# Sinkhorn attention, Fourier mixing and MLP on one core: V cast by its load, f16 means, contiguous e-1 reads, no gate before batch 1, bounded reordering

## The chip, the cores and the metric

The kernel runs on one core of a Trainium2 chip. The metric is the device time in microseconds (us) of one execution. Fast runs of one kernel on one chip mostly agree within 1%. A run that is over 1.5% above the fastest of its kernel is called slow and is not used in a comparison.

TensorE is called PE in the profile (PEld is its weight load), VectorE is DVE, ScalarE is ACT, GpSimd is POOL. "L258" is line 258 of that kernel's own source, so the same operation has different line numbers in different kernels.

## The reference, cut to what matters

```python
# B=4 batches, H=8 heads, S=768 positions, D=64, 8 blocks of 96
P = sort_net
for _ in range(5):                                   # Sinkhorn
    P = np.exp(P - P.max(-1, keepdims=True))
    P = P / P.sum(-1, keepdims=True)
    P = P / P.sum(-2, keepdims=True)
k_sorted = einsum('bhij,bhjcd->bhicd', P, k_blocks)  # blocks mixed by P
v_sorted = einsum('bhij,bhjcd->bhicd', P, v_blocks)
attn = softmax(q_block @ k_sorted_block.T / 8)       # inside each block
x = (attn @ v_sorted)                                # -> [B, 768, 512]
u = x + real(fft(fft(x, axis=1), axis=2))            # over positions, then columns
un = (u - mean(u)) / sqrt(var(u) + 1e-6)
out = u + relu(un @ w1) @ w2                         # 512 -> 2048 -> 512
```

(... the normalisers' 1e-9 and the casts are cut.)

## The kernel before

All of it is one instruction stream that Python generators record piece by piece; a scheduler then orders the instructions on each engine. One generator does the attention of the four batches, one the FFT and normalisation, one the MLP, and one prepares V of batches 2 and 3. V is handled by pairs of batches: 128 partitions are 2 batches x 8 heads x 8 blocks.

The kernel attends with e-1 in place of e = exp(score) and adds V's mean back by other paths, so it needs, for each pair of batches, V in f16 (`vcx`) and the sum of V over the 96 keys of a block ("the means").

V of the first pair comes as f32 over the sync queue, is summed by f32 matmuls and cast by ScalarE:

```python
v32 = [...]                                   # two f32 tiles, 48 keys each
for n in range(4):
    hf, qq = divmod(n, 2)
    start(nc.sync.dma_start(v32[hf][:, 24 * qq:24 * qq + 24, :],
                            vv[0:128, 24 * n:24 * n + 24, :]))
vcx = const.tile([128, 128, D], F16, name="vcx")
dtab = vcx[:, 96:112, :]...                   # a table lives in vcx's spare rows
vcp = vcx[:, 0:BLK, :].rearrange("p (r c) d -> p c r d", r=6)

def v_mean0(n):                               # 12 of these
    nc.tensor.matmul(psm..., idf, v32[n // 6][...], start=(n == 0), stop=(n == 11))

def v_cast(src, n):                           # 8 of these
    nc.scalar.copy(vcp[:, 2 * n:2 * n + 2], src.rearrange("p (c r) d -> p c r d", r=6))
```

The second pair is loaded later, again as f32, cast by ScalarE and summed by VectorE:

```python
def v1_gen():
    for hf in range(2):
        sv = wt([128, 48, D], F32, "hrB", 1, "v32")
        start(nc.gpsimd.dma_start(sv, vv[128:256, 48 * hf:48 * hf + 48]))
        ...
        for n in range(4):
            v_cast(sv[:, 12 * n:12 * n + 12, :], 4 * hf + n)
        ...                                   # VectorE halves sv by additions
    vb_make(1, ...)
    ...
    for n in range(16):
        v_mix(1, n)                           # the second mixing
```

The scores of a block pair are exponentiated into `ex`, and e-1 is written from there into the tile that the next matmul reads. `ex` is in one key order, the destination in another, so e-1 reads `ex` in steps of 16 elements:

```python
nc.scalar.activation(ex..., pss[h2]..., AF.Exp, scale=SCALE)
src = ex.rearrange("p j r c -> p j c r")
if pick(t, 0.5, 0.5) == "DVE":
    nc.vector.tensor_scalar(ed, src, -1.0, None, op0=ALU.add)
else:
    nc.scalar.activation(ed, src, AF.Identity, bias=negone[0:96])
```

A gate holds batch 1's attention until batch 0's second half is normalised:

```python
def attn_gen(k0):
    for b in range(B):
        while b == 1 and not gate1():         # gate1(): (0, 1) in uns
            yield None
        yield from attn(b, k0 if b == 0 else None)
```

One load that turns out to matter is in both kernels: `lt2`, a table of 97 partitions of 3 KB, comes over the sync queue with the other tables, after the Sinkhorn's sixth step.

```python
start(nc.sync.dma_start(tab, ...)); start(nc.sync.dma_start(dtab, ...))
start(nc.sync.dma_start(cs, ...))
lt2 = const.tile([97, 2, S], F16, name="lt2")
start(nc.sync.dma_start(lt2, cn["lt"].ap()))
```

The softmax here doesn't subtract the row's maximum and nothing guards it: scores larger than these inputs give would overflow.

Of the kernel before, what the change touches and what calls it, by code (L numbers as in the profile page):

```python
# [20 lines left out]
D = 64  # L21
# [79 lines left out]
def kernel(  # L101
# [98 lines left out]
    load_qk(0, 0)  # L200
    load_qk(0, 1)
    pack = const.tile([128, 240], F32, name="pack")
# [9 lines left out]

    vv = v.rearrange("b h (i c) d -> (b h i) c d", i=NB)
    v32 = []
    for hf in range(2):
        v32.append(wt([128, 48, D], F32, "hr" + "AB"[hf], 1, "v32"))
    for n in range(4):
        hf, qq = divmod(n, 2)
        start(nc.sync.dma_start(v32[hf][:, 24 * qq:24 * qq + 24, :],
                                vv[0:128, 24 * n:24 * n + 24, :]))  # L220

    vcx = const.tile([128, 128, D], F16, name="vcx")
    dtab = vcx[:, 96:112, :].rearrange("p (c w) d -> p c (w d)", c=4)
    vcp = vcx[:, 0:BLK, :].rearrange("p (r c) d -> p c r d", r=6)

# [7 lines left out]
    for n in range(NKS):  # L233
        t = const.tile([128, NB, 8, 16], F16, name=f"ksb{n}")
        start(nc.gpsimd.memset(t[:, :, 6:8, :], 0.0))
        ksb.append(t)
# [17 lines left out]
    pwt = pw.rearrange("p i j -> p j i")  # L254
    psm = pm([128, 8, D])

    def v_mean0(n):
        nc.tensor.matmul(  # L258
            psm.rearrange("p c d -> p (c d)"), idf,
            v32[n // 6][:, 8 * (n % 6):8 * (n % 6) + 8, :].rearrange(  # L260
                "p c d -> p (c d)"), start=(n == 0), stop=(n == 11))
        op("PE", 0.86)

    def v_cast(src, n):
        nc.scalar.copy(vcp[:, 2 * n:2 * n + 2],  # L265
                       src.rearrange("p (c r) d -> p c r d", r=6))
        op("ACT", 0.86, clk["PE"])

    def v_cast0(n):
        hf, qq = divmod(n, 4)  # L270
        v_cast(v32[hf][:, 12 * qq:12 * qq + 12, :], n)

# [9 lines left out]

    for n in range(6):
        v_mean0(n)

    ph = []
    for it in range(5):
        if it == 0:
            nc.vector.tensor_reduce(rmax, pw, axis=AX.X, op=ALU.max)
            nc.vector.tensor_tensor(  # L290
                pw, pw, rmax[:, :, None].broadcast_to([32, NB, NB]),
                op=ALU.subtract)
        nc.scalar.activation(pw, pw, AF.Exp)
        if it > 1:
            v_cast0(it - 2)
        for src, bc in ((pw, rs[:, :, None]), (pwt, rs[:, None, :])):
            nc.vector.tensor_reduce(rs, src, axis=AX.X, op=ALU.add)
            nc.vector.reciprocal(rs, rs)
            ph.append(nc.vector.tensor_tensor(
                pw, pw, bc.broadcast_to([32, NB, NB]), op=ALU.mult))  # L300
# [29 lines left out]
    def make_bdk(b):  # L330
# [15 lines left out]
        pw[:, :, None, :].broadcast_to([32, NB, 16, NB]))  # L346
    q_copy(0, 0)
    psk = pm([128, NB, 32])
    for i in range(NB):
# [15 lines left out]
    def kq(b, hp):  # L365
# [4 lines left out]
        for half in range(2):  # L370
            ps = pf([128, 3, 128])
            for r3 in range(3):
                r = 3 * half + r3
                for h2 in range(2):
                    nc.tensor.matmul(
                        ps[64 * h2:64 * h2 + 64, r3, :],
                        k16[:, 2 * hl + h2, r, :],
                        bdk[b][:, 2 * hp + h2].rearrange("p i c -> p (i c)"))
            t = op("PE", 0.2)
            t1 = evac(ks[:, :, 3 * half:3 * half + 3, :].rearrange(  # L380
                "p i r c -> p r i c"),
                ps.rearrange("p r (i c) -> p r i c", c=16), t, 384)
        qr, tq = qrs[b, hp]
# [10 lines left out]
    def scores(ks, qt, g, es):  # L394
        pss = [pf([128, 4, BLK]) for _ in range(2)]
        for j in range(4):
            cc = slice(16 * (4 * g + j), 16 * (4 * g + j) + 16)
            for h2 in range(2):
                rows = slice(64 * h2, 64 * h2 + 64)
                nc.tensor.matmul(  # L400
                    pss[h2][:, j, :],
                    ks[rows, 4 * g + j].rearrange("p r c -> p (r c)"),
                    qt[rows, :, cc])
        t = op("PE", 0.36)
        exs = []
        for h2 in range(2):
            ex = wt([96, 4, 6, 16], F32, "ex", 3)
            nc.scalar.activation(
                ex.rearrange("p j r c -> p (j r c)"),
                pss[h2][0:96].rearrange("p j q -> p (j q)"), AF.Exp,  # L410
                scale=SCALE)
            exs.append((ex, op("ACT", 0.5, t)))
        ts = []
        for h2 in range(2):
            e = es[h2]
            ed = bass.AP(
                tensor=e.tensor, offset=e[:, S * g:S * g + 1].offset,
                ap=[e[0:96, :].ap[0], [224, 4], [6, 16], [1, 6]])
            ex, t = exs[h2]
            src = ex.rearrange("p j r c -> p j c r")  # L420
            if pick(t, 0.5, 0.5) == "DVE":
# [354 lines left out]
    def mlp(b):  # L776
        for g in range(2):
# [3 lines left out]
            yield max(t, 62.0)  # L781
            if (b, g) == (0, 1):
                while not v1ok[0]:
                    yield None
            hr = wt([128, 16, GT], F16, "hr" + "AB"[g], 1)
            for fc in range(16):
# [88 lines left out]

    v1ok = [False]

    def v1_gen():
        part = const.tile([128, 2, 3, D], F32, name="vpart")
        for hf in range(2):  # L880
            sv = wt([128, 48, D], F32, "hrB", 1, "v32")
            start(nc.gpsimd.dma_start(sv, vv[128:256, 48 * hf:48 * hf + 48]))
            while clk["PE"] < 62.0 + 8.0 * hf:
                yield None
            for n in range(4):
                v_cast(sv[:, 12 * n:12 * n + 12, :], 4 * hf + n)
                yield clk["PE"] + 0.8
            w = 24
            while w > 3:
                nc.vector.tensor_tensor(sv[:, 0:w], sv[:, 0:w],  # L890
                                        sv[:, w:2 * w], op=ALU.add)
                op("DVE", 0.1 + w * D / 960.0, clk["PE"])
                w //= 2
                yield clk["PE"] + 0.8
            nc.vector.tensor_tensor(part[:, hf], sv[:, 0:3], sv[:, 3:6],
                                    op=ALU.add)
        vb_make(1, part.rearrange("p a c d -> p (a c) d"))
        op("DVE", 0.9)
        v1ok[0] = True
        while 1 not in attnd:  # L900
# [19 lines left out]

    def gate1():
        m = 3
        return (True, (0, 0) in uns, 0 in rowsd, (0, 1) in uns, ndone[0] >= 1,
                ndone[0] >= 3, ndone[0] >= 5, ndone[0] >= 6)[m]

    ndone = [0]

    def attn_gen(k0):
        for b in range(B):
            while b == 1 and not gate1():  # L930
                yield None
            yield from attn(b, k0 if b == 0 else None)
# [17 lines left out]
    for n in range(6, 12):  # L950
        v_mean0(n)
    for n in range(3, 8):
        v_cast0(n)
    k0[0] = sc(k0[0])
# [27 lines left out]
    with ExitStack() as later:  # L982
        for ins in last.values():
            later.enter_context(tc.issue_after(ins))
        go()


# [28 lines left out]
```

## Time and profile before

| | before |
|---|---|
| time, median of 3 runs (range) | 348.93 us (346.69 to 351.01) |
| span of the profiled run | 345.4 us |
| PE busy | 302.8 us (88%) |
| DVE / ACT busy | 208.1 us (60%) / 149.3 us (43%) |

The table of stretches of the kernel before gives, for each stretch (start:end, length), the busy time of each engine and its number of instructions, then the granted TensorE clock as a share of full speed, the busy share of the DMA engines (over 1 where packets overlap) and GB/s:

```profile
...
core 0: us, PE busy (x) PEld busy (x) DVE busy (x) ACT busy (x) POOL busy (x), PEclk, DMA share, GB/s
60.00:80.00 20.00, 10.47 (x90) 7.70 (x90) 14.48 (x29) 8.67 (x16) 0.58 (x2) 0.75 0.75 172
80.00:100.00 20.00, 12.79 (x60) 7.08 (x59) 14.36 (x30) 8.58 (x13) 3.68 (x9) 0.73 0.22 79
100.00:120.00 20.00, 20.00 (x169) 10.73 (x168) 10.66 (x22) 10.82 (x23) 1.62 (x2) 1.00 0.32 53
...
```

From 100 us on PE has almost no gap; in the 40 us before that it works 10 to 13 us of every 20, at a clock of about 0.74. What must change to save time is before 100 us.

The timeline of the kernel before shows that early chain. Columns: start, duration, engine, line, operation, output<-inputs, shape, count, and in brackets the idle time before it with what ended it:

```profile
...
22.40 7.04 PE L258 MATMUL pm_110<-v_81,pack 128*128 128x512 f32 x12
...
29.38 0.21 PE L400 MATMUL pf_229<-qt_216,ksb_92 64*128 64x96 f16 x1
...
73.32 3.03 ACT L265 CAST vcx<-v_530 128x768 f16<-128x768 f32 x4 [6.57 <-DMA v_530<-in_v_dram]
...
76.89 0.49 ACT L678 ACTIVATE y_833<-pf_826 128x386 f16<-128x386 f32 x1
...
87.08 3.03 ACT L265 CAST vcx<-v_901 128x768 f16<-128x768 f32 x4 [8.54 <-DMA v_901<-in_v_dram]
...
90.01 0.81 ACT L715 ACTIVATE un_951<-u_883,nm_915,ny_914 128x512 f16<-128x512 f32 x1
...
95.41 1.49 PE L789 MATMUL pm_1000<-ut_946,w1sb 128*128 128x384 f16 x4
...
```

The second six f32 means (7.04 us; the trace has two records for each of these matmuls) stand in PE's queue directly before the first scores (29.38). Later ScalarE's queue stands 6.57 us at a cast that waits for the second V load; behind it, in the same queue, is the copy of batch 0's first spectrum (76.89). It stands again, 8.54 us, for the other half, ahead of batch 0's first normalised tile (90.01). The first MLP matmul starts at 95.41.

### The profile page before, as it was taken

To read this page: it belongs to the slowest core of one execution; us is meant where nothing else is said; L and a number is where in the kernel's file an instruction comes from. 1 tells how busy PE (TensorE), PEld (TensorE's weight loads), DVE (VectorE), ACT (ScalarE), POOL (GpSimd) and SP (SyncE) were. 2 spreads that over 40 slices of the span, in tenths; PEclk is the share of its full clock that TensorE was granted. 3 is DMA by queue.
4 is the path that set the end of the run, shared out by engine and by line. 5 is a ranking of instruction groups with operands and counts; after the bars stand their busy time and mean duration, and the time that the engine had idled before them with its cause. 6 is when DMAs were issued, how large, how long until landed. Compare 5 with 4: busy or idle time off the path is not lost.

```text
span 345.4 us, 5986 instructions
## 1 busy us (share of the span) xinstructions
PE 302.8 (88%) x2444; PEld 185.7 (54%) x2444; DVE 208.1 (60%) x453; ACT 149.3 (43%) x275; POOL 35.6 (10%) x71
## 2 busy tenths in 40 slices
PE   1758877457399999999999999999999999999995
PEld 0335866344265477876665655765465455554552
DVE  6432678947855468767368754788451374673641
ACT  2345746350746359997743964505016012120000
POOL 7201104000110110012100100020010010010000
PEclk9968799868589999999999999999999999999999
DMA  7999923935000715060921021002102102212002
GB/s 224 337 244 180 181 47 40 225 161 184 0 0 2 134 53 91 2 94 3 134 77 42 3 47 61 32 0 47 61 32 47 61 32 46 81 33 86 31 2 91
DMA packets 26580, 28.05 MB, mean 81 GB/s; under 512 B 10964, under 2 KB 21716, under 8 KB 26294
## 3 DMA queue, kind: packets, MB, share of 16 engines
q0 software_dynamic: 11424, 13.63, 22.0%
q1 hardware_dynamic: 15128, 14.04, 12.9%
q8 instruction: 19, 0.31, 0.4%
q14 instruction: 9, 0.07, 0.1%
HBM read 29.10 MB, written 6.29 MB: 102 GB/s over the span
## 4 chain that ended last, share of the span: by engine, by line
issue 47%; PE 28%; DMA 12%; POOL 5%; DVE 3%; ACT 3%; POOLq 0%; DVEq 0%; ACTq 0%
DMA q_72<-in_q_dram 5%; DMA v_530<-in_v_dram 4%; PE pm_110 L258 2%; DMA v_901<-in_v_dram 2%; ACT vcx L265 1%; PE pm_4048 L806 1%; PE pm_3673 L806 1%; PE pm_4010 L806 1%; PE pm_3856 L806 1%; PE pm_3643 L806 1%; PE pm_3509 L806 1%; PE pm_4029 L806 1%; PE pm_3894 L806 1%; PE pm_3875 L806 1%; PE pm_3479 L806 1%
## 5 line engine op out<-in xcount | busy, mean ns | idle before, releaser
L789 PEld LDWEIGHTS <-w1sb 128*128 128x128 f16 x512 | 49.1, 99 | 34.7 <-issue 4.6
L496 PEld LDWEIGHTS <-vcx 128*128 128x128 f16 x128 | 20.0, 172 | 0.9
L445 PEld LDWEIGHTS <-eb_87 97*128 97x128 f16 x384 | 17.8, 97 | 2.6 <-ACT eb_87 L425 0.8
L258 PE MATMUL pm_110<-v_80,pack 128*128 128x512 f32 x12 | 7.8, 816 | 7.3 <-DMA v_80<-in_v_dram 7.3
L258 PEld LDWEIGHTS pm_110<-v_80,pack 128*128 128x128 f32 x12 | 3.1, 271 | 11.1 <-issue 11.1
L498 PEld LDWEIGHTS <-vbn_309 128*128 128x128 f16 x64 | 8.6, 135 | 0.8 <-DVE vbn_309 L487 0.4
L498 PEld LDWEIGHTS <-vbn_957 128*128 128x128 f16 x64 | 8.3, 130 | 0.3
L806 PEld LDWEIGHTS <-hrB_3913 128*128 128x128 f16 x48 | 4.7, 98 | 5.5
L806 PEld LDWEIGHTS <-hrA_3749 128*128 128x128 f16 x48 | 4.7, 98 | 5.5
L806 PEld LDWEIGHTS <-hrB_3545 128*128 128x128 f16 x48 | 4.7, 98 | 5.5
L806 PEld LDWEIGHTS <-hrA_3276 128*128 128x128 f16 x48 | 4.7, 97 | 5.6
L806 PEld LDWEIGHTS <-hrB_3069 128*128 128x128 f16 x48 | 4.7, 98 | 5.4
L806 PEld LDWEIGHTS <-hrB_1521 128*128 128x128 f16 x48 | 4.6, 99 | 5.4 <-issue 0.2
L400 PEld LDWEIGHTS <-ksb_94 64*128 64x128 f16 x128 | 4.2, 99 | 5.7 <-issue 2.2
L806 PEld LDWEIGHTS <-hrA_2438 128*128 128x128 f16 x48 | 4.5, 98 | 5.0
L806 PEld LDWEIGHTS <-hrA_999 128*128 128x128 f16 x48 | 4.5, 97 | 5.0
L258 PE MATMUL pm_110<-v_81,pack 128*128 128x512 f32 x12 | 7.0, 748 | 0.0
L265 ACT CAST vcx<-v_901 128x768 f16<-128x768 f32 x4 | 3.0, 828 | 8.5 <-DMA v_901<-in_v_dram 8.5
L732 PE MATMUL pf_960<-pack,un_951 128*128 128x128 f16 x4 | 0.6, 307 | 6.4 <-ACT un_951 L715 6.4
L400 PEld LDWEIGHTS <-ksb_92 64*128 64x128 f16 x128 | 3.7, 94 | 4.4 <-issue 3.4
L890 DVE TENSOR_TENSOR v_530<-v_530 128x1536 f32<-128x1536 f32 (+2 forms) x3 | 3.3, 1087 | 4.4 <-ACT vcx L265 4.4
L798 ACT ACTIVATE hrB_3913<-pm_3914 128x384 f16<-128x384 f32 x1 | 0.5, 491 | 12.5 <-PE pm_3914 L789 12.5
(1310 smaller groups left out, 864.6 us busy)
## 6 DMA issues: line engine op xcount, KB each, us to landing
w1sb<-in_moe_w_ch_dram POOLq DMA_DIRECT2D x4, 512.0 KB, 26.7
w2sb<-in_moe_w_ch_dram POOLq DMA_DIRECT2D x4, 512.0 KB, 14.8
v_80<-in_v_dram SPq DMA_DIRECT2D x2, 768.0 KB, 5.5
v_81<-in_v_dram SPq DMA_DIRECT2D x2, 768.0 KB, 11.5
v_530<-in_v_dram POOLq DMA_DIRECT2D x1, 1536.0 KB, 13.3
v_901<-in_v_dram POOLq DMA_DIRECT2D x1, 1536.0 KB, 6.5
cs<-k_cs SPq DMA_DIRECT2D x1, 579.0 KB, 10.0
tab<-k_tab SPq DMA_DIRECT2D x1, 514.0 KB, 7.6
```

Source lines behind the costliest of these rows:

```text
L258: nc.tensor.matmul(psm.rearrange("p c d -> p (c d)"), idf, v32[n // 6][:, 8 * (n % 6):8 * (n % 6) + 8, :].rearrange("p c d -> p (c d)"), s ...
L265: nc.scalar.copy(vcp[:, 2 * n:2 * n + 2], src.rearrange("p (c r) d -> p c r d", r=6))
L400: nc.tensor.matmul(pss[h2][:, j, :], ks[rows, 4 * g + j].rearrange("p r c -> p (r c)"), qt[rows, :, cc])
L445: nc.tensor.matmul(po[:, 65 * T:65 * T + 96], e[:, S * g + 256 * tt + 128 * n: S * g + 256 * tt + 128 * n + 128], vsf[:, vi:vi + 96], star ...
L496: nc.tensor.matmul(ps[:, dd, :], vcx[:, :, d], bd, start=True, stop=False)
L498: nc.tensor.matmul(ps[:, dd, :], vbn[t][:, d:d + 1].broadcast_to([128, 128]), bd, start=False, stop=True)
L732: nc.tensor.matmul(ps[:, c, :], un[:, 128 * c:128 * c + 128], idh, is_transpose=True)
L789: nc.tensor.matmul(ps, w1sb[:, c, 128 * fc:128 * fc + 128], ut[:, c, :], start=(c == 0), stop=(c == 3))
L798: nc.scalar.activation(hr[:, fc, :], ps, AF.Relu)
L806: nc.tensor.matmul(ps, hr[:, fc, 128 * tt:128 * tt + 128], w2sb[:, fc, :], start=(fc == 0), stop=(fc == 15))
L890: nc.vector.tensor_tensor(sv[:, 0:w], sv[:, 0:w], sv[:, w:2 * w], op=ALU.add)
```

## The change

The intent: no engine should cast V, the means should cost little, ScalarE's e-1 should be cheaper, and batch 1's attention should fill the idle stretch before 100 us. Five parts:

1. V is loaded by the GpSimd queue, which casts f32 to f16, directly into `vcx`, in a key order that K and e-1 share. Its packets become 384 bytes.
2. The means are 12 f16 matmuls for each pair.
3. exp writes `ex` in the final key order (its PSUM input is now read in steps), so e-1 reads and writes contiguously.
4. The gate is gone.
5. New ordering edges: on ScalarE and VectorE no instruction may be moved ahead of the one recorded 8 places before it, on PE 64 places.

The last part names 64 and 8; the Trainium skill ("TensorE: Matmul & The Clock Gate", section "Architectural detail: the array is 16× 32×32, not 1× 128×128") gives the same figures as queue depths.

```diff
-        start(nc.sync.dma_start(v32[hf][...], vv[0:128, 24 * n:24 * n + 24, :]))   # x4
+    vv = v.rearrange("b h (i c g r) d -> (b h i) c g (r d)", i=NB, g=2, r=3)
+    def load_v(t):
+        for g in range(2):
+            start(nc.gpsimd.dma_start(
+                vcx[:, 48 * g:48 * g + 48, :].rearrange("p (c r) d -> p c (r d)", r=3),
+                vv[128 * t:128 * t + 128, :, g, :]))
+    load_v(0)                         # after the first k and q, before the second
@@ means and casts
-    def v_mean0(n): ...   def v_cast(src, n): ...   def v_cast0(n): ...
-    for n in range(6):
-        v_mean0(n)
+    def v_mean(psm, n):
+        nc.tensor.matmul(psm..., idh, vcx[:, 8 * n:8 * n + 8, :]..., ...)
+    for n in range(6):                # before the transposes of P; six more before the scores
+        v_mean(psm, n)
@@ exp and e-1
-            ex = wt([96, 4, 6, 16], F32, "ex", 3)
+            ex = wt([96, 4, BLK], F32, "ex", 3)
-                ex.rearrange("p j r c -> p (j r c)"),
-                pss[h2][0:96].rearrange("p j q -> p (j q)"), AF.Exp,
+                ex.rearrange("p j (c r) -> p j c r", r=6),
+                pss[h2][0:96].rearrange("p j (r c) -> p j c r", c=16), AF.Exp,
@@ second pair
     def v1_gen():
-        ... two f32 loads, 8 casts, VectorE sums ...
+        load_v(1)
+        while (0, 0) not in uns:
+            yield None
+        ps = pm([128, 8, D])
+        for n in range(12):
+            v_mean(ps, n)
+        vb_make(1, ps)
@@ gate and bound
-            while b == 1 and not gate1():
-                yield None
+    W = (64, 8, 8)
+    for e, w in zip((EN.PE, EN.DVE, EN.Activation), W):
+        for n in range(w, len(runs[e])):
+            dep(runs[e][n], runs[e][n - w])
```

(... K's layout, which follows the same key order, and the buffers of `hr` are cut, and with them a wait: before, the second pair's f32 V stood in one of the MLP's two `hr` buffers, so the MLP's second group of batch 0 had to wait until V was cast and summed.)

More of the change, by code (lines that the diff above doesn't have):

```diff
@@ L200 @@
     load_qk(0, 0)
-    load_qk(0, 1)
     pack = const.tile([128, 240], F32, name="pack")
@@ L211 @@
     sgn = cm[:, 33:34]
-    vv = v.rearrange("b h (i c) d -> (b h i) c d", i=NB)
-    v32 = []
-    for hf in range(2):
-        v32.append(wt([128, 48, D], F32, "hr" + "AB"[hf], 1, "v32"))
-    for n in range(4):
-        hf, qq = divmod(n, 2)
-        start(nc.sync.dma_start(v32[hf][:, 24 * qq:24 * qq + 24, :],
-                                vv[0:128, 24 * n:24 * n + 24, :]))
     vcx = const.tile([128, 128, D], F16, name="vcx")
     dtab = vcx[:, 96:112, :].rearrange("p (c w) d -> p c (w d)", c=4)
-    vcp = vcx[:, 0:BLK, :].rearrange("p (r c) d -> p c r d", r=6)
+    vv = v.rearrange("b h (i c g r) d -> (b h i) c g (r d)", i=NB, g=2, r=3)
+    def load_v(t):
+        for g in range(2):
+            start(nc.gpsimd.dma_start(
+                vcx[:, 48 * g:48 * g + 48, :].rearrange(
+                    "p (c r) d -> p c (r d)", r=3),
+                vv[128 * t:128 * t + 128, :, g, :]))
+    load_v(0)
+    load_qk(0, 1)
     NE = 4
@@ L233 @@
     for n in range(NKS):
-        t = const.tile([128, NB, 8, 16], F16, name=f"ksb{n}")
-        start(nc.gpsimd.memset(t[:, :, 6:8, :], 0.0))
+        t = const.tile([128, NB, 128], F16, name=f"ksb{n}")
+        start(nc.gpsimd.memset(t[:, :, BLK:128], 0.0))
         ksb.append(t)
@@ L254 @@
     pwt = pw.rearrange("p i j -> p j i")
-    psm = pm([128, 8, D])
-    def v_mean0(n):
+    def v_mean(psm, n):
         nc.tensor.matmul(
-            psm.rearrange("p c d -> p (c d)"), idf,
-            v32[n // 6][:, 8 * (n % 6):8 * (n % 6) + 8, :].rearrange(
-                "p c d -> p (c d)"), start=(n == 0), stop=(n == 11))
-        op("PE", 0.86)
-    def v_cast(src, n):
-        nc.scalar.copy(vcp[:, 2 * n:2 * n + 2],
-                       src.rearrange("p (c r) d -> p c r d", r=6))
-        op("ACT", 0.86, clk["PE"])
-    def v_cast0(n):
-        hf, qq = divmod(n, 4)
-        v_cast(v32[hf][:, 12 * qq:12 * qq + 12, :], n)
+            psm.rearrange("p c d -> p (c d)"), idh,
+            vcx[:, 8 * n:8 * n + 8, :].rearrange("p c d -> p (c d)"),
+            start=(n == 0), stop=(n == 11))
+        op("PE", 0.22)
     qrs = {}
@@ L293 @@
         nc.scalar.activation(pw, pw, AF.Exp)
-        if it > 1:
-            v_cast0(it - 2)
         for src, bc in ((pw, rs[:, :, None]), (pwt, rs[:, None, :])):
@@ L347 @@
     q_copy(0, 0)
+    psm = pm([128, 8, D])
+    for n in range(6):
+        v_mean(psm, n)
     psk = pm([128, NB, 32])
@@ L379, in kq @@
             t = op("PE", 0.2)
-            t1 = evac(ks[:, :, 3 * half:3 * half + 3, :].rearrange(
-                "p i r c -> p r i c"),
-                ps.rearrange("p r (i c) -> p r i c", c=16), t, 384)
+            t1 = evac(ks[:, :, 48 * half:48 * half + 48].rearrange(
+                "p i (c r) -> p i c r", r=3),
+                ps.rearrange("p r (i c) -> p i c r", c=16), t, 384)
         qr, tq = qrs[b, hp]
@@ L401, in scores @@
                     pss[h2][:, j, :],
-                    ks[rows, 4 * g + j].rearrange("p r c -> p (r c)"),
+                    ks[rows, 4 * g + j],
                     qt[rows, :, cc])
@@ L417, in scores @@
                 tensor=e.tensor, offset=e[:, S * g:S * g + 1].offset,
-                ap=[e[0:96, :].ap[0], [224, 4], [6, 16], [1, 6]])
-            ex, t = exs[h2]
-            src = ex.rearrange("p j r c -> p j c r")
+                ap=[e[0:96, :].ap[0], [224, 4], [1, BLK]])
+            src, t = exs[h2]
             if pick(t, 0.5, 0.5) == "DVE":
@@ L781, in mlp @@
             yield max(t, 62.0)
-            if (b, g) == (0, 1):
-                while not v1ok[0]:
-                    yield None
-            hr = wt([128, 16, GT], F16, "hr" + "AB"[g], 1)
+            hr = wt([128, 16, GT], F16, "hr", 2)
             for fc in range(16):
@@ L874, in add @@
         gens.append([prio, gen, None])
-    v1ok = [False]
     def v1_gen():
-        part = const.tile([128, 2, 3, D], F32, name="vpart")
-        for hf in range(2):
-            sv = wt([128, 48, D], F32, "hrB", 1, "v32")
-            start(nc.gpsimd.dma_start(sv, vv[128:256, 48 * hf:48 * hf + 48]))
-            while clk["PE"] < 62.0 + 8.0 * hf:
-                yield None
-            for n in range(4):
-                v_cast(sv[:, 12 * n:12 * n + 12, :], 4 * hf + n)
-                yield clk["PE"] + 0.8
-            w = 24
-            while w > 3:
-                nc.vector.tensor_tensor(sv[:, 0:w], sv[:, 0:w],
-                                        sv[:, w:2 * w], op=ALU.add)
-                op("DVE", 0.1 + w * D / 960.0, clk["PE"])
-                w //= 2
-                yield clk["PE"] + 0.8
-            nc.vector.tensor_tensor(part[:, hf], sv[:, 0:3], sv[:, 3:6],
-                                    op=ALU.add)
-        vb_make(1, part.rearrange("p a c d -> p (a c) d"))
-        op("DVE", 0.9)
-        v1ok[0] = True
+        load_v(1)
[5 more added lines that the diff above has]
+        vb_make(1, ps)
+        op("DVE", 0.9, clk["PE"])
         while 1 not in attnd:
@@ L919, in a_gen @@
             rowsd[2 * t + 1] = clk["PE"] + 5.0
-    def gate1():
-        m = 3
-        return (True, (0, 0) in uns, 0 in rowsd, (0, 1) in uns, ndone[0] >= 1,
-                ndone[0] >= 3, ndone[0] >= 5, ndone[0] >= 6)[m]
     ndone = [0]
@@ L929, in attn_gen @@
         for b in range(B):
-            while b == 1 and not gate1():
-                yield None
             yield from attn(b, k0 if b == 0 else None)
@@ L950 @@
     for n in range(6, 12):
-        v_mean0(n)
-    for n in range(3, 8):
-        v_cast0(n)
+        v_mean(psm, n)
     k0[0] = sc(k0[0])
@@ L984 @@
             later.enter_context(tc.issue_after(ins))
+        n0 = len(traced())
         go()
+    runs = {}
+    W = (64, 8, 8)
+    for ins in traced()[n0:]:
+        if ins.engine in last:
+            runs.setdefault(ins.engine, []).append(ins)
+    for e, w in zip((EN.PE, EN.DVE, EN.Activation), W):
+        for n in range(w, len(runs[e])):
+            dep(runs[e][n], runs[e][n - w])
 _INS = ['q', 'k', 'v', 'sort_net', 'moe_w_ch1', 'moe_w_ch2']
```

## The prediction

> **What bounds the kernel now.** Two regimes. By the table of stretches, the tensor engine is filled from 97 us to 341 us (over 95% busy, clock 1.00). Before that it has 4 to 8 us of work per 10 and its granted clock falls to 0.63-0.84: this stretch is a chain. The Trainium skill ("TensorE: Matmul & The Clock Gate", Part 1) says that idleness throttles the clock; the trace agrees: 256-column matmuls step 0.43 us at 79 us, 0.21 at 83.
>
> In the timeline: q lands at 20.0; the second six f32 mean matmuls (7.0 us) stand from 22.4 to 29.4 before the first scores; V mixing runs 36-47; batch 0's attention ends at 64.7; ScalarE's queue then stands 6.6 us for the second V load (lands 73.3), casts for 3 us and writes the first spectrum only at 76.4, though its matmuls ended near 69; the second half of that V costs another 8.5 us of waiting, 1-2 us of it on the chain. The first MLP matmul is at 95.4. A gate makes batch 1's attention wait for all this.
>
> **What changes.** Removed: 16 ScalarE casts (12.3 us), VectorE sums of V (7.5 us), 14.8 us of f32 mean matmuls; added: 24 f16 ones, about 0.22 us each. e-1 writes on ScalarE took 0.95 us against 0.48 for exps of equal size; contiguous I estimate 0.6, 10 us less ScalarE in all. The exps now read PSUM in steps; spectrum copies do so at 0.49 us, so I expect no penalty. V's load moves to the software queue behind the first k and q, in 384-byte packets. Packets of 768 and 1,024 bytes there took 79 and 98 ns; extrapolated, 50 ns: 13 us for 4,096 packets over 16 engines. Behind k and q, sharing with tables, V lands near 24-25 us. The means stand before the sinkhorn's transposes and before the scores: scores near 27 instead of 29.4.
>
> The larger gain: without the gate, batch 1's attention (9-10 us of matmuls, 30 us of vector work) runs inside batch 0's FFT and normalisation, where the tensor engine idled. The new instruction order has 186 of the 192 attention-times-V matmuls of batches 0 and 1 before the first MLP matmul.
>
> **The sum.** First MLP matmul near 93-95, hardly earlier, but with batch 1's attention done. V's second mixing ends (157 us before) when VectorE has done about 54 us and ScalarE 49 us of work after the first; at 70% use, about 119-121 us. After that the new order holds 194 us of matmuls against 170 before. Before took 184 us for its 170; so 207-208 us now, plus 4 us of tail. Span near 331, time 332.
>
> **Prediction: 332 us, 80% range 321 to 343. Faster by over 2%: 0.83; within 2%: 0.14; slower: 0.03.**
>
> **What would show it.** Right: first scores at 25-29 us; the first spectrum written within 12 us of the end of batch 0's attention; clock above 0.9 from 60 to 100 us; second mixing done by about 120 us; tensor engine filled from there on; ScalarE e-1 near 0.6 us, exp still 0.49. Wrong: V landing after 30 us, its packets at 80-100 ns; exps at 0.8 us or more; second mixing after 135 us.
>
> **What would make it wrong.** Small packets or contention making V late: up to 8 us lost. Exps slowed by stepped PSUM reads: 25 us more ScalarE work where the vector engines now bind. Batch 1's attention delaying batch 0's chain more than it fills. The bound on reordering idling the tensor engine in later mixed stages. On the other side, a denser middle would bring 320.

## The result and the profile after

| | before | after |
|---|---|---|
| median, runs of the first comparison | 348.72 us (4 runs) | 334.36 us (fast runs 332.32, 334.05, 334.66; one slow run) |
| ratio, fast runs | | 0.9567 (0.9481 to 0.9653) |

Ratios are the mean time of one kernel's fast runs over the mean of the other's fast runs of the same rounds, with a 95% interval, so they are not quite the ratio of the medians quoted. The changed kernel is 4.3% faster.

One of its four runs took 802.83 us, and the profile taken with this comparison is of that run. In it every matmul is slow. The groups of the slow run, and then of a fast run of the same kernel (columns: busy us, mean ns of one, idle before), show the MLP's second matmul:

```profile
...
L790 PE MATMUL pm_3461<-w2sb,hr_3258 128*128 128x512 f16 x16 | 10.3, 839 | 0.0
...
```

```profile
...
L790 PE MATMUL pm<-w2sb,hr 128*128 128x512 f16 x384 | 87.0, 379 | 1.4 <-DVE hr L778 1.4
...
```

These 512-column matmuls took 839 ns against 379, while the clock listed for the slow run was 1.00, and the vector engines were not slower (DVE 206.0 us busy against 200.3). No other run of this kernel or a variant did this (one run of `front_both` was slow in a milder way), so the run says nothing about the change and its profile is set aside. The same kernel was run again, under the label `again`: 333.68 us (332.86 to 333.90), ratio 0.9512 (0.9457 to 0.9566), all fast. "After" below is that run, span 331.9 us, with PE 292.5, DVE 200.3 and ACT 122.2 us busy.

The table of stretches of the changed kernel, columns as before:

```profile
...
core 0: us, PE busy (x) PEld busy (x) DVE busy (x) ACT busy (x) POOL busy (x), PEclk, DMA share, GB/s
60.00:80.00 20.00, 14.70 (x187) 10.95 (x185) 17.27 (x41) 11.49 (x27) 3.72 (x4) 0.83 1.41 202
80.00:100.00 20.00, 18.51 (x222) 13.56 (x221) 15.12 (x40) 15.21 (x30) 4.77 (x10) 1.00 0.37 52
100.00:120.00 20.00, 19.26 (x276) 16.29 (x275) 15.59 (x37) 18.28 (x40) 1.62 (x2) 1.00 0.28 41
...
```

PE now works 33.2 us of the 40 from 60 to 100 us (23.3 before). The timeline of the changed kernel shows where the same steps came to stand:

```profile
...
12.87 2.72 PE L257 MATMUL pm<-vcx,pack 128*128 128x512 f16 x6 [12.87 <-DMA vcx<-in_v_dram]
...
28.21 2.72 PE L257 MATMUL pm<-vcx,pack 128*128 128x512 f16 x6 [10.58 <-DMA vcx<-in_v_dram]
...
30.86 0.82 PE L388 MATMUL pf<-qt,ksb 64*128 64x96 f16 x16
...
71.22 0.48 ACT L665 ACTIVATE y<-pf 128x386 f16<-128x386 f32 x1
...
85.12 1.68 PE L257 MATMUL pm<-vcx,pack 128*128 128x512 f16 x7
...
86.46 1.52 ACT L702 ACTIVATE un<-u,nm,ny 128x512 f16<-128x512 f32 x2
...
94.22 0.81 PE L773 MATMUL pm<-ut,w1sb 128*128 128x384 f16 x4
...
```

| step (us) | before | after |
|---|---|---|
| first scores | 29.38 | 30.86 |
| first mixing of V starts | 35.74 | 38.30 |
| batch 0's attention ends | 64.68 | 64.65 |
| first spectrum written | 76.89 | 71.22 |
| first normalised tile | 90.01 | 86.46 |
| first MLP matmul | 95.41 | 94.22 |
| last matmul of the second mixing starts | 157.1 | 115.8 |
| last MLP matmuls end | 341.4 | 328.1 |

Two things stand out. The gain is made where it was forecast: the first MLP matmul is hardly earlier, but by 116 us batch 1's attention and the second mixing are done as well. And the front, which was to win 2 to 3 us, lost 1.5: PE stood 10.58 us, until 28.21, at the second six means, waiting for V.

### The profile page after: what moved, and what is told of

Its sections match the earlier page's. It is cut to its first block, busy times and chain, and to the rows that moved or that the text cites. A ratio compares the mean times of both kernels' runs of the same rounds, so it can differ in the third digit from the quotient of the medians.

```text
span 800.9 us, 5937 instructions
## 1 busy us (share of the span) xinstructions
PE 772.6 (96%) x2444; PEld 366.4 (46%) x2444; DVE 206.0 (26%) x450; ACT 127.7 (16%) x254; POOL 38.8 (5%) x73
## 4 chain that ended last, share of the span: by engine, by line
PE 95%; DMA 3%; DVE 1%; POOL 0%; issue 0%; ACT 0%; POOLq 0%
DMA vcx<-in_v_dram 3%; PE pm_1289 L257 1%; PE pm_4011 L790 1%; PE pm_3015 L790 1%; PE pm_4030 L790 1%; PE pm_3857 L790 1%; PE pm_3838 L790 1%; PE pm_3655 L790 1%; PE pm_3625 L790 1%; PE pm_3461 L790 1%; PE pm_3419 L790 1%; PE pm_3209 L790 1%; PE pm_3179 L790 1%; PE pm_2336 L790 1%; PE pm_2306 L790 1%; PE pm_2112 L790 1%
## 5 line engine op out<-in xcount | busy, mean ns | idle before, releaser
L773 PEld LDWEIGHTS <-w1sb 128*128 128x128 f16 x512 | 90.4, 179 | 133.2 <-issue 132.2
L432 PEld LDWEIGHTS <-eb_83 97*128 97x128 f16 x384 | 53.1, 188 | 9.4 <-issue 9.2
L483 PEld LDWEIGHTS <-vcx 128*128 128x128 f16 x128 | 32.1, 252 | 5.1 <-issue 3.4
L257 PE MATMUL pm_167<-vcx,pack 128*128 128x512 f16 x12 | 9.9, 1095 | 19.6 <-DMA vcx<-in_v_dram 19.6
L257 PEld LDWEIGHTS <-pack 128*128 128x128 f16 x24 | 4.9, 208 | 29.1 <-issue 25.8
L790 PEld LDWEIGHTS <-hr_3258 128*128 128x128 f16 x48 | 9.0, 188 | 19.3 <-issue 19.3
L790 PEld LDWEIGHTS <-hr_3051 128*128 128x128 f16 x48 | 8.7, 181 | 19.9 <-issue 19.9
L790 PEld LDWEIGHTS <-hr_2208 128*128 128x128 f16 x48 | 8.6, 178 | 20.0 <-issue 20.0
L790 PEld LDWEIGHTS <-hr_3527 128*128 128x128 f16 x48 | 8.4, 175 | 20.2 <-issue 20.2
L790 PEld LDWEIGHTS <-hr_3895 128*128 128x128 f16 x48 | 8.4, 174 | 20.0 <-issue 20.0
L790 PEld LDWEIGHTS <-hr_3731 128*128 128x128 f16 x48 | 8.2, 172 | 20.1 <-issue 20.1
L790 PEld LDWEIGHTS <-hr_1372 128*128 128x128 f16 x48 | 8.5, 179 | 19.0 <-issue 19.0
L485 PEld LDWEIGHTS <-vbn_1305 128*128 128x128 f16 x64 | 13.6, 212 | 2.1 <-issue 1.9
L485 PEld LDWEIGHTS <-vbn_297 128*128 128x128 f16 x64 | 13.9, 217 | 0.5
L790 PEld LDWEIGHTS <-hr_2420 128*128 128x128 f16 x48 | 7.0, 155 | 14.2 <-issue 13.4
L388 PEld LDWEIGHTS <-ksb_88 64*128 64x128 f16 x128 | 6.5, 126 | 12.5 <-issue 12.5
L388 PEld LDWEIGHTS <-ksb_90 64*128 64x128 f16 x128 | 6.7, 134 | 8.3 <-issue 7.3
L740 PEld LDWEIGHTS <-lt_152 97*128 97x128 f16 x24 | 6.7, 280 | 8.1 <-issue 8.1
L257 PE MATMUL pm_1289<-vcx,pack 128*128 128x512 f16 x12 | 10.4, 1082 | 0.0
L790 PE MATMUL pm_3491<-w2sb,hr_3258 128*128 128x512 f16 x16 | 10.4, 858 | 0.0
L790 PE MATMUL pm_3461<-w2sb,hr_3258 128*128 128x512 f16 x16 | 10.3, 839 | 0.0
L654 PEld LDWEIGHTS <-pmt 128*128 128x128 f16 x48 | 8.8, 191 | 3.3 <-issue 0.4
## 6 DMA issues: line engine op xcount, KB each, us to landing
vcx<-in_v_dram POOLq DMA_DIRECT2D x4, 768.0 KB, 14.9
```

Source lines behind the costliest of these rows:

```text
L257: nc.tensor.matmul(psm.rearrange("p c d -> p (c d)"), idh, vcx[:, 8 * n:8 * n + 8, :].rearrange("p c d -> p (c d)"), start=(n == 0), stop= ...
L388: nc.tensor.matmul(pss[h2][:, j, :], ks[rows, 4 * g + j], qt[rows, :, cc])
L432: nc.tensor.matmul(po[:, 65 * T:65 * T + 96], e[:, S * g + 256 * tt + 128 * n: S * g + 256 * tt + 128 * n + 128], vsf[:, vi:vi + 96], star ...
L483: nc.tensor.matmul(ps[:, dd, :], vcx[:, :, d], bd, start=True, stop=False)
L485: nc.tensor.matmul(ps[:, dd, :], vbn[t][:, d:d + 1].broadcast_to([128, 128]), bd, start=False, stop=True)
L654: nc.tensor.matmul(ps[pr, n, :], (fo if ci < 2 else fq)[:, ci % 2, 3 * n + t, :] if ci >= 0 else ee[:, 3 * n + t, 128:129], tab[:, t, NK * ...
```

## The experiments

Twelve kernels were run, all correct. They were sent in four calls, and each call timed the kernel before on its own chip. That kernel's median was 347.72 to 351.09 us from call to call, while the changed kernel had 334.36 and 333.68, so a comparison across calls is good to about 1%: where one matters, the text gives it both by the times and by the ratios to before. The diffs are against the changed kernel unless stated.

### The same kernel again

> The changed kernel once more, for a profile in the fast state (the one profile so far fell in a run of 803 us, in which every matmul was slow). My account: 334 us; first scores at 25-29 us; V landed by 25 us; second V mixing ended by about 120 us; clock above 0.9 from 60 to 100 us; tensor engine filled from there on. Rival, that the gain comes from the later stages and not from a denser middle: second mixing ends after 130 us.

Measured: 333.68 us, as above.

### e-1 in its old order

```diff
-            ex = wt([96, 4, BLK], F32, "ex", 3)     # exp reorders, e-1 contiguous
+            ex = wt([96, 4, 6, 16], F32, "ex", 3)   # exp contiguous, e-1 reads in steps
```

> The changed kernel with the exps written as they lie in PSUM and the e-1 step reading them in steps, as before; the instruction order on all engines is the same as in the changed kernel. My account: ScalarE's e-1 goes from 0.61 back to 0.95 us for 38 of them, 13 us of ScalarE work, but only half lies in the stretch where the vector engines bind and it is shared with VectorE: 2 to 4 us slower. Rival, that ScalarE alone paces the middle: 6 us or more. Second rival, that its waits are elsewhere: under 1 us.

Measured: 337.25 us (336.18 to 338.72), ratio 0.9621, against 333.68 on the same chip. The order of the instructions on PE, DVE and ACT is the same in both, so this isolates the access order. Groups of `strided_e1` and then of the changed kernel (busy us, mean ns of one):

```profile
...
L413 ACT ACTIVATE eb<-ex,negone 96x384 f16<-96x384 f32 x38 | 36.2, 966 | 0.4
L396 ACT ACTIVATE ex<-pf 96x384 f32<-96x384 f32 x64 | 28.6, 496 | 22.8 <-PE pf L388 22.7
...
L410 DVE TENSOR_SCALAR eb<-ex 96x384 f16<-96x384 f32 x26 | 13.9, 536 | 21.7 <-ACT ex L396 21.3
...
```

```profile
...
L396 ACT ACTIVATE ex<-pf 96x384 f32<-96x384 f32 x64 | 28.5, 494 | 24.4 <-PE pf L388 24.3
L412 ACT ACTIVATE eb<-ex,negone 96x384 f16<-96x384 f32 x38 | 23.4, 629 | 0.4
...
L409 DVE TENSOR_SCALAR eb<-ex 96x384 f16<-96x384 f32 x26 | 9.4, 364 | 20.5 <-ACT ex L396 20.0
...
```

ScalarE's e-1 goes from 966 to 629 ns in these group means, and exp, which took over the stepped reading, stays at 494 (496): a stepped read costs here when ScalarE reads SBUF, and not when it reads PSUM. VectorE's e-1 became cheaper too, from 536 to 364 ns, which was not forecast. Together 17.3 us less work on the vector engines is worth 3.6 us of time, within the 2 to 4 forecast.

### The gate put back

```diff
+            while b == 1 and not gate1():
+                yield None
             yield from attn(b, k0 if b == 0 else None)
```

> The changed kernel with the gate on batch 1's attention put back, nothing else. My account: moving batch 1's attention into batch 0's FFT and normalisation carries most of the gain, so with the gate 8-10 us are lost: 342-344 us, and the first MLP matmul comes about 10 us earlier than without it. Rival, that the V load is what pays (no casts and no waiting in ScalarE's queue): within 2 us of 334.

Measured: 348.58 us (348.18 to 350.05), ratio 0.9950: the whole gain is gone, which is more than either theory allowed. The timeline of `gate_back` shows that it isn't only the gate:

```profile
...
67.59 0.49 ACT L665 ACTIVATE y<-pf 128x386 f16<-128x386 f32 x1 [0.89 <-PE pf L654]
...
72.94 1.86 PE L257 MATMUL pm<-vcx,pack 128*128 128x512 f16 x4 [5.39 <-DMA vcx<-in_v_dram]
...
75.81 0.49 ACT L665 ACTIVATE y<-pf 128x386 f16<-128x386 f32 x1 [7.73 <-PE pf L654]
...
77.01 1.02 PE L257 MATMUL pm<-vcx,pack 128*128 128x512 f16 x4 [0.38 <-DMA vcx<-in_v_dram]
...
```

The scheduler has moved the means of the second pair of batches forward on PE, in between the matmul groups of batch 0's FFT. PE, whose matmuls keep their order, stands 5.39 us for V's second load, and the second spectrum is copied 8.2 us after the first. In the changed kernel the same twelve matmuls stand at 85.12, where V's last packet (78.1 in the trace) had landed 7 us before. So this run puts back the gate and a V wait at once, and can't say what the gate alone is worth.

### The bound on reordering taken out

```diff
-    for e, w in zip((EN.PE, EN.DVE, EN.Activation), W):
-        for n in range(w, len(runs[e])):
-            dep(runs[e][n], runs[e][n - w])
```

> The changed kernel without the bound on reordering, so that the scheduler may move any instruction of the later section. My account gave it no term of its own: within 3 us of 334 either way. Rival, that the bound keeps the mixed middle dense and carries a good part of the gain: 340 us or more, with idle tensor engine between 70 and 200 us.

Measured: 351.45 us (350.69 to 354.51), ratio 1.0039: again no gain left, which is the rival's side (340 us or more). The timeline of `no_bound`:

```profile
...
76.15 2.72 PE L257 MATMUL pm<-vcx,pack 128*128 128x512 f16 x6 [8.83 <-DMA vcx<-in_v_dram]
...
80.21 1.46 PE L257 MATMUL pm<-vcx,pack 128*128 128x512 f16 x6 [1.34 <-DMA vcx<-in_v_dram]
...
84.62 0.48 ACT L665 ACTIVATE y<-pf 128x386 f16<-128x386 f32 x1
...
```

The means of the second pair now stand even before batch 0's first FFT matmul: PE waits 8.83 us and then 1.34 us, and the first spectrum is written at 84.62 instead of 71.22. The change took V's wait out of ScalarE's queue; without the bound it reappears in PE's.

### Both again, with these twelve means pinned

To take the V wait out of both, the twelve matmuls were tied behind batch 0's third output tile of the FFT, about where the changed kernel has them.

```diff
+            dep(v_mean(ps, n).ins, mark[0].ins)     # mark: batch 0's third output-DFT group
```

Without the bound:

> No bound on reordering, but V's second-half means (batches 2 and 3) may not pass the third output-DFT group of batch 0 in the tensor engine's queue. In the run without the bound those 12 matmuls stood ahead of batch 0's first FFT matmul and held the queue for their load, 8.8 us and 1.3 us. Account: the bound pays only because it keeps these 12 behind; so 334 to 338 us, first MLP matmul at 95-100 us. Rival, that the bound itself keeps the middle dense: 346 us or more.

With the gate:

> The gate put back, with the same pin on V's second-half means. In the run with the gate they held the tensor engine's queue from 67.5 to 72.9 us. Account: the gate by itself costs what batch 1's attention is worth in matmul time, 8-10 us: 341-344 us, the first MLP matmul at about 86-89 us instead of 95. Rival, that the gate only mattered through the place of the means: 334 to 336 us.

Measured: 339.38 us (338.81 to 340.73), ratio 0.9758, and 339.42 us (338.72 to 340.24), ratio 0.9747. So of the 14.9 us that putting the gate back cost, 9.2 by the times (7 by the ratios) were V's wait in PE's queue, and 5.7 (8) are the gate's own. Of the 17.8 us that the bound was worth, 12.1 (10) came back with the pin, and 5.7 (9) are something else. These come from another call than the unpinned runs, hence the two figures. With the gate the pin moved hardly anything but the means (ScalarE's order is unchanged). Without the bound it changed the order of other instructions on all three engines as well, so the 12.1 us can't all be put down to the V wait. Both times lie between account and rival; the first MLP matmuls, at 99.65 us without the bound and 86.89 us with the gate, are where the accounts had them.

The timeline of `no_bound_means_pinned` shows some of what is left:

```profile
...
83.04 0.36 DVE L268 COPY qr<-q 128x768 f16<-128x768 f16 x1 [3.84 <-DMA q<-in_q_dram]
...
```

VectorE's queue stands 3.84 us at a copy of q that was moved ahead of batch 0's normalisation and whose load has not landed. The first normalised tile is at 91.16 us there, 4.7 us later than after the change. The bound, by its construction, keeps an instruction on PE, VectorE or ScalarE from being moved further ahead than its 64 or 8 places. That such waits make up the rest of its worth is not shown.

### V's part undone

The kernel before with contiguous e-1, no gate and the bound, so the f32 loads, casts and f32 means remain.

```diff
 (against the kernel before)
+            ex = wt([96, 4, BLK], F32, "ex", 3)     # exp and e-1 as in the change
-            while b == 1 and not gate1():
-                yield None
+            dep(runs[e][n], runs[e][n - w])         # the bound
```

> V loaded, cast and averaged as before (f32 load, ScalarE casts, f32 means), with the other parts of the change kept: contiguous e-1, no gate, reordering bound. Theory (the gate could only be dropped at a gain because no engine queue stands on V's second load any more): ScalarE's queue stands 6-8 us twice on V's second load between 62 and 90 us, batch 0's first spectrum is late as before, the second mixing ends at 125-135 us, median 338-345 us, at most a third to a half of the whole gain. Rival (dropping the gate with the bound is nearly the whole gain, V's part is worth little): median 333-337 us, second mixing ends before 122 us.

Measured: 345.18 us (344.57 to 346.00), ratio 0.9866. The whole change has 0.9512 to 0.9567, so without V's part about 70% of it is lost: the theory's side, with a median just beyond its range. The detail was partly wrong. The timeline of `v_old`:

```profile
...
71.32 0.83 ACT L265 CAST vcx<-v 128x768 f16<-128x768 f32 x1 [5.55 <-DMA v<-in_v_dram]
...
88.72 3.01 ACT L265 CAST vcx<-v 128x768 f16<-128x768 f32 x4
...
93.50 0.83 ACT L714 ACTIVATE un<-u,nm,ny 128x512 f16<-128x512 f32 x1
...
```

ScalarE stood once, 5.55 us, and not twice: at the second half (88.72) other work had kept it busy until V was there. The first normalised tile is at 93.50, 7 us later than after the change: the first spectrum, at 74.32, is 3.1 us late, and GpSimd starts the normaliser's small operations at 89.50 instead of 84.59, 4.9 us late. The second mixing's last matmul starts at 130.3. "V's part" here includes the MLP's wait for the second V, named above under the change.

### The gate alone taken from the kernel before

```diff
 (against the kernel before)
-            while b == 1 and not gate1():
-                yield None
```

> The kernel before with the gate alone removed, nothing else changed. Theory (the gate was there for a reason: without V's new load and without the bound, batch 1's attention delays batch 0's chain): within 1% of before, 346-352 us; batch 0's first spectrum later than 76.9 us. Rival (the gate alone was the fault of the old kernel): 338-343 us.

Measured: 353.83 us (350.87 to 354.20), ratio 1.0084 (0.9993 to 1.0174): no gain, perhaps a small loss, with the first spectrum at 79.24 us. Dropping the gate pays only together with the other parts.

### Where the front's time went: the means last

The next runs ask why the scores came at 30.86 us. First, all twelve means of the first pair were put behind the second group of scores.

```diff
-    for n in range(6, 12):
-        v_mean(psm, n)            # before the scores
     k0[1] = sc(k0[1])
+    for n in range(12):
+        v_mean(psm, n)
```

> The changed kernel with V's first twelve means moved behind the second pair of scores, so that neither the sinkhorn's transposes nor the first scores wait for V in the tensor engine's queue. V's second half still lands near 28 us. Account: V mixing then starts near 33 us instead of 38.3, all later work moves up by 5 us, 328-330 us. Rival, that something behind hides the front: over 332 us.

Measured: 325.85 us (324.50 to 327.33), ratio 0.9357 (0.9303 to 0.9412). The timeline of `means_last`:

```profile
...
17.38 0.82 PE L385 MATMUL pf<-qt,ksb 64*128 64x96 f16 x16 [0.65 <-DVE qt L375]
...
24.82 2.74 PE L257 MATMUL pm<-vcx,pack 128*128 128x512 f16 x6
...
27.79 1.46 PE L257 MATMUL pm<-vcx,pack 128*128 128x512 f16 x6 [0.22 <-DMA vcx<-in_v_dram]
...
```

Scores start 13.5 us earlier. The mixing needs the means and starts at 29.08 instead of 38.30, so 9 us of the front are won, better than forecast (mixing near 33 us, 328 to 330 us in all), and the whole kernel is faster than the changed kernel by 7.8 us in times, 1.6% (5.4 us) by the ratios to before (0.9357 against 0.9512).

### The large tables after V

```diff
-    start(nc.sync.dma_start(tab, ...)) ... dtab, cs, lt2, rb2    # after the Sinkhorn's sixth step
+    gated(nc.sync.dma_start(tab, ...), last_v_mean)              # after the second V half is read
```

> The changed kernel with the table loads of the sync queue issued only after the last of V's first means. Account: V's packets of 384 bytes take the 51 ns they should, but share each DMA engine in turn with the larger packets of the tables; alone, V's second half lands at 19-21 us instead of 28.2, the first scores come at 22-24 us, and 326-329 us follow. Rival, that V's small packets are slow in themselves: V still lands after 26 us, and nothing is gained.

Measured: 328.25 us (326.99 to 328.36), ratio 0.9417. The timeline of `tables_late`:

```profile
...
17.77 2.74 PE L257 MATMUL pm<-vcx,pack 128*128 128x512 f16 x6
...
20.44 0.52 PE L376 MATMUL pf<-qt,ksb 64*128 64x96 f16 x16
...
32.55 0.32 PE L471 MATMUL pm<-bdv,vcx 128*128 128x128 f16 x1 [6.38 <-DMA vcx<-k_dtab]
...
```

The second six means run at 17.77 without a wait: V lands over 10 us earlier when no table shares the DMA engines. Scores are at 20.44. Part of this was given back: the mixing reads the tile in which `dtab` lives, so it waited 6.38 us for the delayed table.

### Both, with `dtab` left early

```diff
+    for n in range(12):
+        gate_v = v_mean(psm, n)                        # after the second scores
+    gated(nc.sync.dma_start(tab, ...), gate_v)         # then cs, lt2, rb2; dtab stays early
```

> The changed kernel with all 12 of the first V means queued behind the second score group (as in means_last) and the large tables except dtab held until those means have run (as in tables_late); dtab alone stays early, because the mixing reads the tile it lies in. Theory (two separate faults at the front: means queued ahead of the scores, and V sharing the DMA engines with tables): V's second half lands by 20 us, scores end by 17.5 us, the means run without a wait by 24 us, mixing starts at 26-27.5 us against 29.1 in means_last, median 323-325 us against 325.85. Rival (once the scores are free of the means, V's landing is not on the chain, the mixing is held by the vector engines instead): mixing starts at 28.5 us or later and the median stays within 1 us of 325.85.

Measured: 325.31 us (fast runs 324.31 to 325.36), ratio 0.9287 (0.9213 to 0.9361); the median is within 0.6 us of `means_last`, so the rival holds: with the means out of the way, V's landing isn't what the scores or the mixing wait for. (By the ratios it is 0.7% better, but the intervals overlap.) The profiled run of this kernel was slow, 388.99 us at a recorded clock of 0.765, so nothing of its later stages is compared. Its front runs as in `means_last`, with scores at 17.39 and 24.07 us, and shows what the mixing does wait for:

```profile
...
24.07 0.82 PE L374 MATMUL pf<-qt,ksb 64*128 64x96 f16 x16 [0.65 <-DVE qt L364]
...
24.83 4.56 PE L257 MATMUL pm<-vcx,pack 128*128 128x512 f16 x12
...
```

The means run without any wait for V, and the mixing still starts right behind them, at 29.22 us (29.08 in `means_last`). PE's own queue, the second scores and then the means, sets that start; the rival had put it down to the vector engines, for which only the next matmul waits (1.19 us).

### One table's load split

What in the tables delays V? The page's DMA part, narrowed to stretches of 2 us, gives for each queue the packets, MB and the time of its packets as a share of 16 engines. V is in q0 (software), tables in q1 (hardware). The changed kernel, 12 to 14 us, then 14 to 16 us, then 26 to 28 us:

```profile
...
q0 software_dynamic: 989, 0.38, 156.9%
...
```

```profile
...
q1 hardware_dynamic: 171, 0.58, 80.3%
q0 software_dynamic: 222, 0.09, 34.4%
...
```

```profile
...
q0 software_dynamic: 116, 0.39, 98.6%
q1 hardware_dynamic: 13, 0.04, 5.4%
...
```

From 12 to 14 us V has the engines almost alone: 989 packets, and 3 on q1. From 14 to 16 us the two queues move almost the same number of packets (222 and 171; from 16 to 18 us 207 and 210), so a queue of 384-byte packets gets a share of 0.34 against 0.80. The Trainium skill ("DMA: Bandwidth & Descriptors", section "Queues, rings and completion order") says that each engine takes turns between queues packet by packet, and these counts agree.

This explains a slow stretch until about 20 us, but not 28.2. From 20 us to about 36 us there remains a trickle on q1: 13 packets in 2 us, and 5.4% of 16 engines is 0.86 of one engine. Only `lt` fits: 0.04 MB in 13 packets is 3 KB each, and the list of loads has it at 291 KB, which is 97 such rows. The same page (section "Why a DMA increments its semaphore by 16 and not by 1") says that a load uses the largest number of engines up to 16 that divides its outer dimension. 97 is a prime, which by that rule leaves one engine. V's last packets on that engine would take turns with 3 KB packets, and the wait for V ends with its last packet. The trace's single packets, read one by one, say the same: the 97 packets of 3,072 bytes never overlap and run from 19.3 to 36.0 us, and from 21.5 to 27.6 us each of them is followed by exactly one packet of V, the last at 27.62. The edit:

```diff
-    start(nc.sync.dma_start(lt2, cn["lt"].ap()))
+    start(nc.sync.dma_start(lt2[0:96], cn["lt"].ap()[0:96]))
+    start(nc.sync.dma_start(lt2[96:97], cn["lt"].ap()[96:97]))
```

> The changed kernel with one load written differently: the lt table (97 partitions of 3 KB) as 96 partitions and then 1, instead of 97 at once. Theory (97 has no divisor up to 16, so the whole table goes through one DMA engine; from 20 to 34 us the hardware queue shows a steady trickle of 12 packets in 2 us at 5% of 16 engines, which is 0.8 of one engine, and V's last packets on that engine wait behind it): no such trickle is left, V's second half lands at 20-21.5 us instead of 28.2, first scores at 23-24.5 us instead of 30.9, everything after moves up by 6-8 us, median 325-328.5 us against 333.68. Rival (V is late because tables as a whole take turns with its packets): V's second half lands at 26 us or later, scores no earlier than 29 us, median 332-335 us.

Measured: 327.43 us (326.29 to 328.61), ratio 0.9305 (0.9264 to 0.9347). The DMA part of `lt_split`, 26 to 28 us, has no line for q1 any more, and the timeline shows V's second half:

```profile
...
q0 software_dynamic: 124, 0.44, 110.3%
...
```

```profile
...
22.50 2.72 PE L257 MATMUL pm<-vcx,pack 128*128 128x512 f16 x6 [4.19 <-DMA vcx<-in_v_dram]
...
25.15 0.82 PE L389 MATMUL pf<-qt,ksb 64*128 64x96 f16 x16
...
```

The trickle is gone (the 97 packets now overlap and are through within 2.2 us, by 20.6), V lands at 22.50 instead of 28.21, and the scores start at 25.15. The order of the instructions on PE, DVE and ACT is the same as in the changed kernel, so nothing but this load differs. V was about 1 us later than the theory had it, the time is in its range. This one-line edit is worth 2.2% by the ratios (0.9305 against 0.9512), or 6.3 us in times. Of V's lateness, 5.7 us were the one engine's, and the other 5 us or so (22.5 against at most 17.8 in `tables_late`) the turns taken with the other tables.

`means_last`, `tables_late`, `front_both` and `lt_split` all beat both kernels. The best two by the ratios, `front_both` and `lt_split`, can't be told apart by their intervals; `lt_split` together with `means_last` was not run.

## Why the prediction was right or wrong

The time was right: 332 us forecast, 334.36 and 333.68 measured, and the direction and the main mechanism held. Point by point:

- **V's packets.** Forecast 50 ns for 384 bytes, extrapolated from 79 and 98 ns for larger ones. Measured 51.0 ns on average over 8,192 packets. Right.
- **V lands at 24 to 25 us, scores near 27, a gain of 2 to 3 us at the front.** Wrong, and this is the term that failed: V's second half landed at 28.21 and the scores started at 30.86, a loss of 1.5 us. "Sharing with tables" was in the forecast as a general allowance. What it missed is that the share goes by packets and not by bytes, and that one table went through a single engine until 36 us; `lt_split` recovers 5.7 us of V's landing by undoing only that. That the means stand before the scores was seen, and not followed to its end: `means_last` starts the scores at 17.38 by running the means after them, at 24.82.
- **First spectrum within 12 us of the end of batch 0's attention.** Right: 6.6 us (71.22 against 64.65; before 12.2).
- **The gate is the larger gain.** Right in that it is a gain: by 116 us batch 1's attention and the second mixing are done, and the first MLP matmul is at 94.22 (forecast 93 to 95). In size it was a little less than the 9 to 10 us of matmuls that were to move: the gate's own worth, in `gate_back_means_pinned`, is 5.7 us by the times and 8 by the ratios. Too simple as a cause: `before_no_gate` shows that without the other parts dropping it is worth nothing. That it is the larger gain is not shown: V's part, undone, costs about 11 us.
- **The bound.** It had no term in the sum and stood only among the risks. It is what makes the rest work: without it all is lost (1.0039), and half to two thirds of that comes back when V's means are pinned on PE.
- **ScalarE e-1 at 0.6 us, exp unchanged, no penalty for stepped PSUM reads.** Right: 0.61 to 0.63 us and 0.49 us.
- **Clock above 0.9 from 60 to 100 us.** Half right: 0.83 from 60 to 80 us and 1.00 from 80 to 100 us.
- **Second mixing done by 119 to 121 us, then 207 to 208 us, then 4.** The sum held and both terms were off in opposite directions: its last matmul starts at 115.8 us, 212 us pass until the last MLP matmuls end, then 3.8. The remaining 194 us of matmuls were given the kernel before's absolute surcharge (184 for 170, 14 us); in proportion (184/170) it would have been 210. That the total came out within 2.4 us is thus in part luck: an early middle and a late end cancelled.

Undone one at a time, V's part costs about 11 us, the gate 14.9, the bound 17.8 and e-1 3.6: 47 us for a change worth 15. The parts are conditions of one another. The traces of three of these runs (`gate_back`, `no_bound`, `v_old`) show the same thing come back on one engine or another: a queue that stands at a late V load and holds back the work behind it.

What stays open: what makes up the rest of the bound's own 5.7 to 9 us beyond the 3.84 us seen on VectorE, where the rest of `v_old`'s 7 us comes from beyond the 3.1 at its first spectrum, and what caused the one run of 802.83 us.

## What to carry to other kernels

When you remove a wait, look where the scheduler puts the instruction that waited: on an in-order queue a consumer moved ahead of its load stops everything behind it, whichever engine it is on. Order each engine's queue by when its data lands, and test the parts of a combined change with that order pinned, or you measure the reordering. Before adding a load with small packets, list what else is in flight: it gets turns by packets and not by bytes, and a table with a prime number of partitions, as the 97 here, can keep one DMA engine busy long after the rest.

## What the Trainium skill lacked or had wrong

- "DMA: Bandwidth & Descriptors", "Specifications": it says that below 512 bytes a transfer costs a read-modify-write. No extra cost shows here: 384-byte packets into SBUF took 51.0 ns on average, on the line through 79 ns (768 bytes) and 98 ns (1,024 bytes). These are sizes as written, in f16; V is read as f32, 768 bytes a packet, so a packet that is small on both sides was not tried.
- "DMA: Bandwidth & Descriptors", "Queues, rings and completion order": it has the turns by packet, and not what follows: 222 packets of 384 bytes got 0.34 of 16 engines while 171 larger ones got 0.80. The page's packet typically holds 9 to 17 descriptors; in the trace the turns with `lt` were one packet of 384 bytes for one of 3,072.
- The same page, "Why a DMA increments its semaphore by 16 and not by 1": the rule for the number of engines agrees with the trickle at 0.86 of one engine for a 97-partition load. It lacks the consequence for other queues: V, on another queue, landed 5.7 us later for it, and writing the load as 96 partitions and 1 gained 2.2% of the whole kernel.
- "ScalarE: Activation LUTs", "Step-by-step: what each stage is for": it gives 0.833 ns per element for all functions. The access order counts as well, of which other pages of the skill warn but this one does not: a 384-element e-1 from SBUF took 966 ns read in steps of 16 elements and 629 ns contiguously; an exp from PSUM took 496 and 494 ns.
- "TensorE: Matmul & The Clock Gate", "Seeing it yourself", warns that recorded clock events are unreliable. The run of 802.83 us fits this, without proving it: its profile has no row of the clock at all, the listed clock was 1.00, and 512-column matmuls took 839 ns instead of 379. What the clock really was is not shown.
